# Strassen's method for the down products of two blocks, as a stage at the end of a layer kernel

## The chip, the cores and the metric

The kernel runs on one core of a Trainium2 chip. The metric is the time of one execution on the device in microseconds (us). A profiled execution shows the core's engines: TensorE (PE, with its weight loads as PEld), VectorE (DVE), ScalarE (ACT), GpSimd (POOL) and SyncE (SP), whose queue issues nearly all DMA transfers.

## The reference

One transformer layer on 2048 tokens of 640 features: a normalization, attention in a dilated window, a second normalization and a gated feed-forward layer with 1728 hidden features. Weights and data are float32.

```python
def _B_ref(x, w_gate, w_up, w_down):
    g = _silu(x @ w_gate)
    u = x @ w_up
    return (g * u) @ w_down

x = A_x
h = x + _A_ref(_layernorm(x, axis=-1), A_wqkv, A_wo)
h2 = h + _B_ref(_layernorm(h, axis=-1), B_w_gate, B_w_up, B_w_down)
return h2
```

`_A_ref` projects to queries, keys and values, attends for each token to 8 earlier positions two apart, and projects with `wo`.

## The kernel before, in words

The tokens are cut into four blocks of 512 (b = 0 to 3), the hidden features into 14 tiles of 128 (i = 0 to 13; the last has 64). Every float32 product is made from operands that are split into a high part, rounded for TensorE's faster float32 form (`fp32r`), and a low part, the difference. Three passes are multiplied and added up: high by high, low by high, high by low. A split costs a ScalarE cast (the high part) and a VectorE subtraction (the low part).

A feed-forward tile of one block is: gate and up products (5 chunks x 3 passes x 2 matmuls of 512 columns) into two banks of PSUM, SiLU on ScalarE, a multiply on VectorE, the split of the result (`act_split`), and the down product. The down product of a tile is 5 x 3 matmuls of 512 columns: four banks hold 128 tokens by 512 output features each, the fifth (bank 4) the last 128 features transposed. Banks 0 to 4 are accumulated over all 14 tiles of a block (`Downs` and `down_batch`), and `finish(b)` adds them to the residual `h_t()` and stores the block's output.

Blocks 0 and 1 go tile by tile (`ffn`, `classic`). Blocks 2 and 3 are done together in `pair(early)`, with `early` = 4:

- `wo3` makes block 3's attention output and its normalized input, which is moved into `kv`.
- Tiles 0 to 3 of block 2 are classic ones.
- `sums()` makes sums and differences of the two blocks' inputs. Tiles 4 to 12 are then `pair_tile`s: gate and up of both blocks from seven products in place of eight (Strassen's method over gate/up, the two blocks and two groups of chunks), in banks 5, 6 and 7 in turn. Block 2's activation goes on to its down product; block 3's is stored to the scratch tensor `psc`. `between()` puts a down batch of an earlier tile between the products.
- Tile 13 of block 2 is classic; `finish(2)`.
- For block 3, tiles 13 and 0 to 3 are classic ones. Tiles 4 to 12 are `kept_tile`s: the down weights are loaded again and split, the stored activation is loaded from `psc` and split, and the down product follows. Then `finish(3)`.

The order of all instructions is written out: every operation is recorded with `P.add(engine, cost, function, reads, writes, ...)`, and the table `ORDER` gives, in groups of (engine, first, count), the order in which they are emitted. Each engine executes its own in that order and waits by semaphores for those of others; DMA transfers are issued by SP in its order. The tile `ra` (19200 columns, fp32r) holds wo, weights and, in the pair stage, the sums; `wsl` (the space of `pq`), `kv`, `shb`, `acts` hold weights, block 3's input, block 2's input and the split activations, and `fa` float32 data.

```python
for i in range(early, NF - 1):
    d.put(pair_tile(i, fn[0], lambda: d.pend and d.do()))
    fn[0] += 1
```

## Time and profile before

| what | value |
|---|---|
| median of 3 runs | 850.06 us (847.94 to 850.62) |
| profiled execution | 849.7 us, span 848.0 us |
| TensorE busy | 839.8 us, 3953 matmuls |
| VectorE busy | 706.7 us, 847 instructions |
| ScalarE busy | 415.7 us, 745 instructions |
| DMA | 173.30 MB, mean 204 GB/s |
| HBM | read 126.57 MB, written 44.70 MB |

The span is the time from the first to the last instruction of the profiled execution; the rest of its time lies around it. Busy times are sums of the durations of instructions, and the durations of neighbours on an engine can overlap. The granted clock of TensorE is full in the whole span.

### The profile page before, as it was taken

To read this page: it belongs to the slowest core of one execution; us is meant where nothing else is said; L and a number is where in the kernel's file an instruction comes from. 1 tells how busy PE (TensorE), PEld (TensorE's weight loads), DVE (VectorE), ACT (ScalarE), POOL (GpSimd) and SP (SyncE) were. 2 spreads that over 40 slices of the span, in tenths; PEclk is the share of its full clock that TensorE was granted. 3 is DMA by queue.
4 is the path that set the end of the run, shared out by engine and by line. 5 is a ranking of instruction groups with operands and counts; after the bars stand their busy time and mean duration, and the time that the engine had idled before them with its cause. 6 is when DMAs were issued, how large, how long until landed. Compare 5 with 4: busy or idle time off the path is not lost.

```text
span 848.0 us, 10721 instructions
## 1 busy us (share of the span) xinstructions
PE 839.8 (99%) x3953; PEld 713.1 (84%) x3953; DVE 706.7 (83%) x847; ACT 415.7 (49%) x745; POOL 3.3 (0%) x12
## 2 busy tenths in 40 slices
PE   8999999999999999999999999999999999999998
PEld 7888888889888888887888888888878888888886
DVE  6499999999999999999999999996696667455343
ACT  6856574242872454477444457555553333234232
POOL 0000000000000000000000000000000000000000
PEclk9999999999999999999999999999999999999999
DMA  7897877658989795968999889868413122205332
GB/s 249 249 261 184 273 196 213 160 153 226 297 253 268 247 280 185 272 222 277 267 315 315 284 256 288 247 216 310 145 47 105 60 101 77 87 32 207 130 126 95
DMA packets 87141, 173.30 MB, mean 204 GB/s; under 512 B 33440, under 2 KB 52128, under 8 KB 86320
## 3 DMA queue, kind: packets, MB, share of 16 engines
q1 hardware_dynamic: 85680, 171.96, 66.0%
q10 hardware_dynamic: 1408, 0.66, 0.3%
q8 instruction: 31, 0.51, 0.2%
q14 instruction: 22, 0.18, 0.1%
HBM read 126.57 MB, written 44.70 MB: 202 GB/s over the span
## 4 chain that ended last, share of the span: by engine, by line
PE 72%; DVE 17%; DMA 4%; issue 2%; ACT 2%; SPq 1%; POOL 0%; DVEq 0%; ACTq 0%; POOLq 0%
PE bank L964 20%; PE bank L979 17%; PE bank L671 17%; PE bank L1132 12%; DVE pq L783 3%; DVE pq L742 3%; DVE pq L748 3%; PE bank L876 3%; DVE pq L792 2%; DMA pq<-qsc 2%; PE bank L1209 2%; DMA kv<-fa 1%; DMA kv<-ksc 1%; PE bank L528 1%; DMA ra<-lsc 1%
## 5 line engine op out<-in xcount | busy, mean ns | idle before, releaser
L964 PE MATMUL bank<-shb,ra 128*128 128x512 f32 x930 | 225.1, 390 | 0.1
L964 PEld LDWEIGHTS bank<-shb,ra 128*128 128x128 f32 x930 | 173.4, 188 | 35.7 <-DVE fa L1003 0.6
L979 PE MATMUL bank<-ra,acts 128*128 128x512 f32 x656 | 170.6, 390 | 0.2 <-DVE acts L1015 0.2
L979 PEld LDWEIGHTS bank<-ra,acts 128*128 128x128 f32 x656 | 122.3, 188 | 25.3 <-DVE acts L1015 0.6
L671 PE MATMUL bank<-ra,sha 128*128 128x512 f32 (+2 forms) x480 | 106.5, 380 | 0.2 <-ACT ra L642 0.2
L671 PE MATMUL bank<-ra,shb 128*128 128x512 f32 (+1 forms) x470 | 102.9, 378 | 0.0
L671 PEld LDWEIGHTS bank<-ra,sha 128*128 128x128 f32 x480 | 89.3, 188 | 13.4 <-ACT ra L642 0.5
L671 PEld LDWEIGHTS bank<-ra,shb 128*128 128x128 f32 x470 | 87.9, 188 | 12.7
L742 DVE TENSOR_TENSOR pq<-kv,pq 128x2560 f32<-128x2560 f32 x32 | 90.2, 2820 | 2.3 <-DMA pq<-qsc 1.3
L792 DVE TENSOR_TENSOR pq<-pq 128x1280 f32<-128x1280 f32 (+2 forms) x96 | 89.7, 934 | 2.0
L783 DVE TENSOR_TENSOR pq<-kv,pq 128x2560 f32<-128x2560 f32 x32 | 90.3, 2822 | 0.7
L748 DVE TENSOR_REDUCE pq<-pq 128x128 f32<-128x2560 f32 x32 | 90.0, 2811 | 0.4
L678 ACT ACTIVATE st<-bank,fa 128x480 f32<-128x480 f32 (+3 forms) x120 | 51.1, 473 | 52.3 <-PE bank L671 38.3
L940 DVE TENSOR_TENSOR ra<-fa,ra 128x640 fp32r<-128x640 f32 (+1 forms) x70 | 56.2, 819 | 13.3 <-ACT ra L930 12.1
L993 ACT CAST acts<-fa 128x512 fp32r<-128x512 f32 x52 | 32.1, 619 | 55.0 <-DVE fa L1003 41.6
L930 ACT CAST ra<-fa 128x640 fp32r<-128x640 f32 x56 | 40.4, 726 | 34.8 <-PE bank L979 34.8
L876 PE MATMUL bank<-ra 128*128 128x320 f32 x360 | 55.8, 309 | 0.0
L876 PEld LDWEIGHTS bank<-ra 128*128 128x128 f32 x360 | 54.3, 188 | 1.4
L945 ACT CAST ra<-fa 128x1280 fp32r<-128x1280 f32 (+1 forms) x35 | 42.5, 1216 | 21.9 <-DMA fa<-in_ffn_dram 17.6
L979 PE MATMUL bank<-acts,ra 128*128 128x512 f32 x164 | 45.9, 391 | 0.0
L1002 ACT ACTIVATE fa<-bank 128x512 f32<-128x512 f32 x34 | 20.3, 598 | 50.2 <-PE bank L964 47.0
L1003 DVE TENSOR_TENSOR fa<-bank,fa 128x512 f32<-128x512 f32 x34 | 23.2, 683 | 20.7 <-PE bank L964 10.9
(162 smaller groups left out, 969.4 us busy)
## 6 DMA issues: line engine op xcount, KB each, us to landing
fa<-in_ffn_dram SPq DMA_DIRECT2D x43, 960.0 KB, 6.1
kv<-ksc SPq DMA_DIRECT2D x32, 440.0 KB, 6.2
kv<-vsc SPq DMA_DIRECT2D x32, 440.0 KB, 6.2
ra<-lsc SPq DMA_DIRECT2D x17, 640.0 KB, 6.7
lsc<-ra SPq DMA_DIRECT2D x13, 640.0 KB, 7.1
ra<-lsc SPq DMA_DIRECT2D x19, 320.0 KB, 4.4
ksc<-st SPq DMA_DIRECT2D x32, 160.0 KB, 3.3
pq<-qsc SPq DMA_DIRECT2D x16, 320.0 KB, 6.8
```

The source lines that it names most:

```text
L671: T.matmul(banks[bk][:, 0:n], l, r_(wq(g, w, c) + shift, n), start=(p, c) == first_mm, stop=(p, c) == last_mm)
L678: P.add("ACT", act(m) + 0.06, lambda: A.activation(stage_t()[:, o : o + NJ * m].rearrange("p (t j c) -> p t j c", j=NJ, c=w)[:, :, j, :], ...
L742: P.add("DVE", dve(2560), lambda: V.tensor_tensor(pq(PROD, 2560).rearrange("p (j w c) -> p j w c", j=2, w=W), window(ko, 2 * jp), pq(qo + ...
L748: P.add("DVE", dve(2560), lambda: V.tensor_reduce(logits(lo)[:, :, 16 * jp : 16 * jp + 16].rearrange("p h n -> p n h"), pq(PROD, 2560).rea ...
L783: V.tensor_tensor(pq(PROD, 2560).rearrange("p (j n d) -> p j n d", j=2, d=DH), bass.AP(tensor=v.tensor, offset=v.offset, ap=[list(v.ap[0]) ...
L792: V.tensor_add(dst(v), v[:, :, 0:m, :], v[:, :, m : 2 * m, :])
L876: T.matmul(banks[bk][:, 0:320], l, r_(m, 320), start=p == 0 and c == 0, stop=p == 2 and c == NC - 1)
L940: low(640, lambda E, o=o: E.tensor_sub(ws(t, lo + o, 640)[p0:], fa[p0:, raw + o : raw + o + 640], ws(t, hi + o, 640)[p0:].bitcast(F32)), [ ...
L945: P.add("ACT", act(n), lambda: A.copy(ws(wt, gu, n), f(raw, n)), r=[rf(raw, n)], w=[rws(wt, gu, n)], prio=PR["fh"])
L964: T.matmul(banks[bk], ws(wt, gu + 1280 * w + wid * c + col, 128), x(a, c), start=p == 0 and c == 0, stop=p == 2 and c == NC - 1)
L979: T.matmul(banks[k], l, m, start=first and p == 0, stop=stop and p == len(passes) - 1)
L1132: T.matmul(banks[bk], ws(wt, o + 2048 * w + 128 * k, 128), xv_[k](a), start=first and p == 0 and k == 0, stop=stop and p == 2 and k == n - ...
```

## The change

The down products of eight tiles (4 to 11) of blocks 2 and 3 are taken out of the two blocks' accumulations and become the function `products(paired)` behind `finish(3)`.

- In the pair stage tile 12 now comes first, then the eight paired tiles. A paired tile (`keep`) loads only its gate and up weights, and its block-2 activation is stored to `psc[0]` instead of being split; block 3's goes to `psc[1]`, already in the order of the down product. Only tile 12 remains a `kept_tile`.
- `finish` of blocks 2 and 3 no longer stores the output; the new stage adds to `h_t()` and stores.
- `products` takes tiles in pairs (4 pairs). For each pair, the activations of both blocks form a 2 x 2 scheme (even or odd token rows j by first or second tile; each part 512 tokens by 128 features) and the down weights another (first or second tile by left or right 320 output features). Seven products with eight sums of parts for each pair (four of activations, four of weights) replace eight products. Each product (`m1` to `m7`) runs over the four pairs: `unit` splits one part of activations and one of weights into high and low (in a slot of a buffer that has become free), and `phase` issues 4 banks x 4 pairs x 3 passes of matmuls with 320 columns. `into` adds a bank to the output, and `store` sends it away. The float32 sources lie in `ar` (the first half of `ra`'s space) and `wr` (`shb`'s space); two small memsets on GpSimd mark when these become free.
- `ra` is cut into `ra` and `rb` of 9600 columns each, some offsets move by 128 columns, and `ORDER` is a new table for the whole program.

The diff without `ORDER` (of which two lines are shown) and small changes of names:

```diff
-EARLY = 4
+EARLY, NP = 4, 4
...
-    (2, 0, 1), (4, 2, 1), (3, 1, 1), (3, 0, 1), (4, 10, 1), (2, 7, 1), (1, 0, 1), (0, 0, 1), (4, 4, 1), (4, 3, 1), (1, 14, 1), (0, 1, 1), (0, 9, 1), (4, 5, 1),
+    (3, 1, 1), (3, 0, 1), (2, 0, 1), (0, 0, 1), (1, 0, 1), (4, 2, 1), (4, 7, 1), (2, 7, 1), (4, 4, 1), (0, 1, 1), (1, 10, 1), (4, 6, 1), (4, 5, 1), (0, 7, 1),
...
-        psc = dr.tile([NF, 128, 512], F32, name="psc")
+        psc = dr.tile([2, NF, 128, 512], F32, name="psc")
...
-            lo, hi = (n, n + 640) if cut else (0, n + 640)
+            lo, hi = ((0, n + 640), (n, n + 640), (0, n))[cut]
...
-            down_hi(raw, 1280, dn)
-            down_lo(i, raw, 1280, dn)
+            if not keep:
+                down_hi(raw, 1280, dn)
+                down_lo(i, raw, 1280, dn)
...
-            act_split(Y1, y1, ao, 2)
+            if keep:
+                P.add("SP", 0.45, lambda: Q.dma_start(psc[0, i], Y1()), r=[y1], w=[(f"R{i}", 0, 512)], prio=3, nbytes=nb(128, 2048))
+            else:
+                act_split(Y1, y1, ao, 2)
...
-            d = Downs(NF)
+            paired = list(range(early, early + 2 * NP))
+            others = [i for i in range(early, NF - 1) if i not in paired]
+            d = Downs(NF - 2 * NP)
...
-            for i in range(early, NF - 1):
-                d.put(pair_tile(i, fn[0], lambda: d.pend and d.do()))
+            for i in others + paired:
+                t = pair_tile(i, fn[0], lambda: d.pend and d.do(), i in paired)
+                if i in others:
+                    d.put(t)
                 fn[0] += 1
...
-            for i in range(early, NF - 1):
+            for i in others:
                 d.put(kept_tile(i))
...
             finish(3)
+            products(paired)
+
+        def products(ts):
+            n, m = len(ts), len(ts) // 2
+            S2, T2, Y1 = XN, AB2, AB2 + 1280
+            HN = 320
...
+            U = 1664
+            slots = [(lambda o=o: r_(o, U), [rr(o, U)]) for o in (17536,)]
+            slots += [(lambda o=o: kv[:, o : o + U], kvr(o, U)) for o in (0, U, 2 * U)]
+            slots += [(lambda o=o: r_(o, U), [rr(o, U)]) for o in (9600, 9600 + U)]
+            slots += [(lambda o=o: wsl_t()[:, o : o + U], [rpq(o, U)]) for o in (0, U, 2 * U)]
+            slots += [(lambda o=o: act_t()[:, o : o + U], [("ab", o, o + U)]) for o in (0, U)]
+            slots += [(lambda o=o: r_(o, U), [rr(o, U)]) for o in (13696, 13696 + U)]
+
...
+
+            def acts(s, odd):
+                v = lambda: ar_t()[:, 0 : 1024 * n].rearrange("p (b s jj o t) -> p b s jj o t", b=2, s=n, jj=2, o=2)[:, :, s, :, odd, :]
+                return v, [rr(512 * n * b + 512 * s + 256 * jj + 128 * odd, 128) for b in range(2) for jj in range(2)]
+
+            def wts(s, half):
+                o = 640 * s + HN * half
+                return (lambda: wr_t()[:, o : o + HN]), [("shb", o, o + HN)]
+
+            def s2(p):
+                return (lambda: f(S2 + 512 * p, 512).rearrange("p (b jj t) -> p b jj t", b=2, jj=2)), [rf(S2 + 512 * p, 512)]
+
+            def t2(p):
+                return (lambda: f(T2 + HN * p, HN)), [rf(T2 + HN * p, HN)]
+            P.add("POOL", 0.1, lambda: G.memset(ar_t()[:, RA_C - 2 : RA_C], 0.0), w=[rr(0, RA_C)], prio=0)
+            P.add("POOL", 0.1, lambda: G.memset(wr_t()[:, 0:2], 0.0), w=[("shb", 0, 5120)], prio=0)
+            for s, i in enumerate(ts):
+                for b in range(2):
+                    o = 512 * n * b + 512 * s
+                    P.add("SP", 0.45, lambda i=i, b=b, o=o: Q.dma_start(ar_t()[:, o : o + 512], psc[b, i]), r=[(f"{'RP'[b]}{i}", 0, 512)], w=[rr(o, 512)], prio=PR["fld"], nbytes=nb(128, 2048))
+                P.add("SP", 0.45, lambda i=i, s=s: Q.dma_start(wr_t()[:, 640 * s : 640 * s + 640], ffn_in[i][:, 1280:1920]), w=[("shb", 640 * s, 640 * s + 640)], prio=PR["fld"], nbytes=nb(128, 2560))
+            units = [0]
+
+            def unit(a, w):
+                k = units[0] % len(slots)
+                units[0] += 1
+                (av, ar), (wv, wr) = a, w
+                sv = slots[k][0]
+                for src, sr, o, c in ((av, ar, 0, 512), (wv, wr, 1024, HN)):
+                    hi, lo = (lambda o=o, c=c: sv()[:, o : o + c]), (lambda o=o, c=c: sv()[:, o + c : o + 2 * c])
+                    if c == 512:
+                        shape = lambda v: v.rearrange("p (b jj t) -> p b jj t", b=2, jj=2)
+                    else:
+                        shape = lambda v: v
+                    P.add("ACT", act(c), lambda src=src, hi=hi, shape=shape: A.copy(shape(hi()), src()), r=sr, w=part(k, o, c), prio=1)
+                    P.add("DVE", dve(c), lambda src=src, hi=hi, lo=lo, shape=shape: V.tensor_sub(shape(lo()), src(), shape(hi()).bitcast(F32)), r=sr + part(k, o, c), w=part(k, o + c, c), prio=1)
+                return k
+
+            def phase(us, bk0, first, stop):
+                for tp in range(4):
+                    for p, k in enumerate(us):
+                        def mm(tp=tp, p=p, k=k):
+                            v = slots[k][0]()
+                            for q, (a, w) in enumerate(((0, 0), (1, 0), (0, 1))):
+                                T.matmul(banks[bk0 + tp][:, 0:HN], v[:, 512 * a + 128 * tp : 512 * a + 128 * tp + 128], v[:, 1024 + HN * w : 1024 + HN * w + HN],
+                                         start=first and p == q == 0, stop=stop and p == m - 1 and q == 2, skip_group_check=True)
+                        P.add("PE", 3 * 0.1482, mm, r=part(k, 128 * tp, 128) + part(k, 512 + 128 * tp, 128) + part(k, 1024, 2 * HN), w=[pb(bk0 + tp)], prio=10)
+
+            def sub(o, x, y, add=False):
+                (ov, orr), (xv_, xr), (yv, yr) = o, x, y
+                c = 512 if len(orr) != 1 or orr[0][2] - orr[0][1] == 512 else HN
+                op = V.tensor_add if add else V.tensor_sub
+                P.add("DVE", dve(c), lambda: op(ov(), xv_(), yv()), r=xr + yr, w=orr, prio=1)
+
+            def into(tp, odd, half, bk):
+                b, j = tp // 2, 2 * (tp % 2) + odd
+                lo = 2560 * b + 640 * j + HN * half
+                P.add("DVE", dve(HN), lambda: V.tensor_add(h_t()[:, lo : lo + HN], banks[bk][:, 0:HN], h_t()[:, lo : lo + HN]), r=[pb(bk), ("sha", lo, lo + HN)], w=[("sha", lo, lo + HN)], prio=0.5)
+
+            def store(tp, odd, o, c):
+                b, j = tp // 2, 2 * (tp % 2) + odd
+                lo = 2560 * b + 640 * j + o
+                P.add("SP", 0.45, lambda: Q.dma_start(out[2 + b, :, j, o : o + c], h_t()[:, lo : lo + c]), r=[("sha", lo, lo + c)], prio=3, nbytes=nb(128, 4 * c))
+            ps = range(m)
+            m1 = [unit(acts(2 * p, 0), wts(2 * p, 0)) for p in ps]
+            m2 = [unit(acts(2 * p + 1, 0), wts(2 * p + 1, 0)) for p in ps]
+            phase(m1, 0, True, False)
+            for tp in range(4):
+                b, j = tp // 2, 2 * (tp % 2)
+                y = Y1 + HN * tp
+                P.add("ACT", act(HN), lambda y=y, tp=tp: A.copy(f(y, HN), banks[tp][:, 0:HN]), r=[pb(tp)], w=[rf(y, HN)], prio=0)
+                lo = 2560 * b + 640 * j + HN
+                P.add("DVE", dve(HN), lambda lo=lo, y=y: V.tensor_add(h_t()[:, lo : lo + HN], f(y, HN), h_t()[:, lo : lo + HN]), r=[rf(y, HN), ("sha", lo, lo + HN)], w=[("sha", lo, lo + HN)], prio=1)
+                lo = 2560 * b + 640 * j + 640
+                two = lambda v: v.rearrange("p (a c) -> p a c", a=2)
+                P.add("DVE", dve(640), lambda lo=lo, y=y, two=two: V.tensor_add(two(h_t()[:, lo : lo + 640]), f(y, HN)[:, None, :].to_broadcast([128, 2, HN]), two(h_t()[:, lo : lo + 640])),
+                      r=[rf(y, HN), ("sha", lo, lo + 640)], w=[("sha", lo, lo + 640)], prio=1)
+            phase(m2, 0, False, True)
+            for tp in range(4):
+                into(tp, 0, 0, tp)
+                store(tp, 0, 0, HN)
+            for p in ps:
+                a11, a21, a12, a22 = acts(2 * p, 0), acts(2 * p, 1), acts(2 * p + 1, 0), acts(2 * p + 1, 1)
+                b11, b12, b21, b22 = wts(2 * p, 0), wts(2 * p, 1), wts(2 * p + 1, 0), wts(2 * p + 1, 1)
+                sub(a11, a11, a21)
+                sub(b11, b12, b11)
+                sub(s2(p), a22, a11)
+                sub(t2(p), b22, b11)
+                sub(a21, a21, a22, True)
+                sub(a12, a12, s2(p))
+                sub(b12, b22, b12)
+                sub(b21, b21, t2(p))
+            m6 = [unit(s2(p), t2(p)) for p in ps]
+            phase(m6, 4, True, False)
+            for tp in range(4):
+                into(tp, 0, 1, 4 + tp)
+            m7 = [unit(acts(2 * p, 0), wts(2 * p, 1)) for p in ps]
+            phase(m7, 4, False, False)
+            for tp in range(4):
+                into(tp, 1, 1, 4 + tp)
+            m5 = [unit(acts(2 * p, 1), wts(2 * p, 0)) for p in ps]
+            phase(m5, 0, True, False)
+            for tp in range(4):
+                into(tp, 1, 1, tp)
+            m4 = [unit(acts(2 * p + 1, 1), wts(2 * p + 1, 0)) for p in ps]
+            phase(m4, 4, False, True)
+            for tp in range(4):
+                into(tp, 1, 0, 4 + tp)
+                store(tp, 1, 0, D)
+            m3 = [unit(acts(2 * p + 1, 0), wts(2 * p + 1, 1)) for p in ps]
+            phase(m3, 0, False, True)
+            for tp in range(4):
+                into(tp, 0, 1, tp)
+                store(tp, 0, HN, HN)
...
-                cuts = (0, 256, 512) if b == NB - 1 and j == NJ - 1 else (0, 512)
+                cuts = (0, 512)
...
+                    if b > 1:
+                        continue
```

```

Three places in the order, first TensorE in the middle of the pair stage, before. L1132 are the products of `pair_tile`, L979 down products; bank_74, bank_75 and bank_76 are banks 5, 6 and 7, bank_69 to bank_73 banks 0 to 4.

```order
L1132 MATMUL bank_74<-shb,wsl 128x512 x6
L1132 MATMUL bank_76<-kv,ra 128x512 x6
L979 MATMUL bank_71<-ra,acts 128x512 x3
L1132 MATMUL bank_75<-ra,wsl 128x512 x6
L979 MATMUL bank_73<-acts,ra 128x512 x3
L1132 MATMUL bank_76<-kv,ra 128x512 x3
L1132 MATMUL bank_75<-ra,wsl 128x512 x6
L1132 MATMUL bank_75<-kv,wsl 128x512 x3
```

The same engine and stage after the change, where L1158 are the products of `pair_tile`, and bank_75, bank_76, bank_77 are banks 5, 6 and 7 (bank_70 to bank_74 are banks 0 to 4).

```order
L1158 MATMUL bank_75<-shb,wsl 128x512 x6
L1158 MATMUL bank_76<-ra,wsl 128x512 x6
L1158 MATMUL bank_77<-ra,wsl 128x512 x6
L1158 MATMUL bank_76<-ra,wsl 128x512 x6
L1158 MATMUL bank_76<-kv,wsl 128x512 x3
L1158 MATMUL bank_75<-shb,wsl 128x512 x9
L1158 MATMUL bank_76<-ra,wsl 128x512 x9
L1158 MATMUL bank_75<-shb,rb 128x512 x6
L1158 MATMUL bank_76<-ra,rb 128x512 x6
```

The down products have gone from between; only six matmuls on bank 5 or 7 lie between two uses of bank 6.

TensorE at the passage to the new stage, after the change: L1004 are down products, L1405 the new products, L1482 `finish`'s transposes.

```order
L1004 MATMUL bank_71<-rb,acts 128x512 x3
L1405 MATMUL bank_77<-wsl 128x320 x3
L1004 MATMUL bank_70<-rb,acts 128x512 x3
...
L1004 MATMUL bank_73<-rb,acts 128x512 x6
L1405 MATMUL bank_70<-rb 128x320 x3
L1004 MATMUL bank_74<-acts,rb 128x512 x6
L1405 MATMUL bank_70<-kv 128x320 x3
L1405 MATMUL bank_71<-rb 128x320 x3
L1405 MATMUL bank_71<-kv 128x320 x3
L1482 MATMUL bank_74<-fa 128x128 x4
```

Before, the same engine ended in down products alone:

```order
L979 MATMUL bank_71<-ra,acts 128x512 x6
L1316 MATMUL bank_73<-fa 128x128 x4
L979 MATMUL bank_69<-ra,acts 128x512 x6
L979 MATMUL bank_70<-ra,acts 128x512 x6
L979 MATMUL bank_72<-ra,acts 128x512 x9
```

The new products begin between the last down products of block 3 and go on for 336 matmuls.

VectorE at that passage, after the change: L1396 are the low parts of `unit`, L1413 the sums of parts, L1489 `finish`'s additions, L965 and L1022 the splits of down weights and activations, L1028 the gate-up multiply of a classic tile.

```order
L1028 TENSOR_TENSOR fa<-bank_76,fa 128x512
L1396 TENSOR_TENSOR kv<-ar,kv 128x512
L1413 TENSOR_TENSOR ar<-ar 128x2x2x128
L1396 TENSOR_TENSOR kv<-ar,kv 128x512
L1396 TENSOR_TENSOR kv<-wr,kv 128x320
L1413 TENSOR_TENSOR ar<-ar 128x2x2x128 x2
L965 TENSOR_TENSOR rb<-fa,rb 128x640
L1022 TENSOR_TENSOR acts<-fa,acts 128x4x4x32
L965 TENSOR_TENSOR rb<-fa,rb 128x640
L1022 TENSOR_TENSOR acts<-fa,acts 128x512
L1396 TENSOR_TENSOR rb<-wr,rb 128x320
```

And before, behind the last gate-up multiply (L1003; L997 and L940 split activations and down weights):

```order
L1003 TENSOR_TENSOR fa<-bank_75,fa 128x512
L997 TENSOR_TENSOR acts<-fa,acts 128x4x4x32 x2
L940 TENSOR_TENSOR ra<-fa,ra 128x640
L997 TENSOR_TENSOR acts<-fa,acts 128x4x4x32
L940 TENSOR_TENSOR ra<-fa,ra 128x640
```

Where two splits alternated for each kept tile, the units and sums of the new stage now stand among the splits of the last tiles, and go on behind them.

44 lines of the change are left out of this document (29 added, 15 removed), and 442 rows, old and new, of the table ORDER.

## The prediction

> **What bounds the kernel now.** I read the page first, then the chain that ended last, the windows of the last 250 us, and the groups of that stretch.
>
> ```profile
> span 848.0 us, 10721 instructions
> PE 839.8 (99%) x3953; PEld 713.1 (84%) x3953; DVE 706.7 (83%) x847; ACT 415.7 (49%) x745; POOL 3.3 (0%) x12
> PEclk9999999999999999999999999999999999999999
> PE 72%; DVE 17%; DMA 4%; issue 2%; ACT 2%; SPq 1%; POOL 0%; DVEq 0%; ACTq 0%; POOLq 0%
> ```
>
> TensorE is busy 99% of the span at full granted clock, so its work sets the time, wherever nothing makes it wait. A busy matmul is longer than the step to the next one, because they overlap; the price of a matmul is its share of a run in the chain of waits:
>
> ```profile
> 492.04 2.19 PE bank L876 x15
> 578.02 0.88 PE bank L1209 x6
> 806.29 32.64 PE bank L979 x144
> 838.93 0.44 PE bank L1316 x4
> ```
>
> A 128x512 down product (L979) steps at 32.64 / 144 = 0.2267 us, a 128x320 product (L876) at 2.19 / 15 = 0.1460 us; six of L1209 give 0.147, the same. These two are the terms of the sum.
>
> VectorE is the second engine. It has room only in the late windows (columns: window, length, then busy time and instruction count of PE, PEld, DVE, ACT, POOL):
>
> ```profile
> 650.00:700.00 50.00, 50.00 (x222) 41.32 (x221) 30.52 (x49) 17.14 (x27) 0.00 (x0) 1.00 0.25 89
> 740.00:760.00 20.00, 20.00 (x90) 16.57 (x89) 9.30 (x14) 6.08 (x10) 0.63 (x1) 1.00 0.00 1
> 780.00:800.00 20.00, 20.00 (x89) 16.54 (x89) 8.25 (x12) 6.01 (x8) 0.00 (x0) 1.00 0.49 172
> 820.00:830.00 10.00, 10.00 (x46) 8.29 (x45) 4.31 (x6) 3.75 (x6) 0.00 (x0) 1.00 0.53 173
> ```
>
> From 740 us on, VectorE and ScalarE are busy less than half of the time and the DMA engines about half. That idle time is what the change spends.
>
> **The change, part by part.** *Matmuls removed.* Eight tiles, two blocks, 5 banks x 3 passes: 8 x 2 x 15 = 240 products of 512 columns, 240 x 0.2267 = 54.40 us of TensorE.
>
> *Matmuls added.* Seven products, 4 banks each, 4 pairs of tiles, 3 passes: 7 x 4 x 4 x 3 = 336 of 320 columns, 336 x 0.1460 = 49.06 us. TensorE saves 5.34 us. In columns it is exactly 7/8 (107520 for 122880), but the step is not in proportion to columns: 320/512 of 0.2267 would be 0.1417, so the narrower shape gives back 336 x 0.0043 = 1.4 us. The Trainium skill (TensorE: Matmul & The Clock Gate, "Wait — 56ns, not 53.3ns?") gives a warm step of columns over 2.4 GHz plus about 2.5 ns; by that the saving would be an estimated 240 x 215.8 - 336 x 135.8 ns = 6.2 us. The trace disagrees: its two steps make (0.2267 - 0.1460) / 192 = 0.42 ns a column and a fixed 11 ns, and the rows count.
>
> *Vector and Scalar work removed.* Each of the eight tiles drops, in the pair tile and again in the kept tile, the down weights' cast and difference and the activations' cast and difference:
>
> ```profile
> L940 DVE TENSOR_TENSOR ra<-fa,ra 128x640 fp32r<-128x640 f32 x27 | 21.9, 822 | 13.2 <-ACT ra L930 12.1 <-ACT ra L945 1.1
> L997 DVE TENSOR_TENSOR acts<-fa,acts 128x512 fp32r<-128x512 f32 x26 | 17.8, 688 | 13.7 <-ACT acts L993 13.7
> L930 ACT CAST ra<-fa 128x640 fp32r<-128x640 f32 x28 | 20.1, 724 | 16.6 <-PE bank L979 16.6
> L993 ACT CAST acts<-fa 128x512 fp32r<-128x512 f32 x26 | 16.0, 618 | 16.4 <-PE bank L979 10.1 <-DVE fa L1003 3.0 <-DVE fa L1106 1.8
> L1256 DVE TENSOR_TENSOR h<-bank,h 128x320 f32<-128x320 f32 x8 | 3.9, 485 | 2.7 <-PE bank L1209 2.5
> L1219 ACT COPY fa<-bank 128x320 f32<-128x320 f32 x6 | 2.6, 426 | 7.7 <-PE bank L1209 7.7
> ```
>
> That is 16 x (0.822 + 0.688) = 24.2 us of VectorE and 16 x (0.724 + 0.618) = 21.5 us of ScalarE; none of it was on the path, so it earns nothing by itself.
>
> *Vector and Scalar work added.* 28 units split activations and weights into high and low parts (28 x 512 and 28 x 320 columns on each engine), 32 sums and differences (16 x 512, 16 x 320), and the additions to the result (28 x 320, 4 x 640; ScalarE copies 4 x 320). VectorE: 44 x 0.688 + 72 x 0.485 + 4 x 0.82 = 68.5 us by duration; ScalarE 28 x 0.618 + 32 x 0.426 = 30.9 us. They must run inside the last 100 us, beside TensorE. Whether they fit depends on the step from one VectorE instruction to the next, not on its duration (three pairs in order of time: start, length; then two groups that the pair stage needs below):
>
> ```profile
> 654.20 0.42 DVE L1108 TENSOR_TENSOR fa<-fa 128x256 f32<-128x256 f32 x1
> 654.53 0.69 DVE L997 TENSOR_TENSOR acts<-fa,acts 128x512 fp32r<-128x512 f32 x1
> 785.19 0.82 DVE L940 TENSOR_TENSOR wsl<-fa,wsl 128x640 fp32r<-128x640 f32 x1
> 785.92 0.69 DVE L1003 TENSOR_TENSOR fa<-bank,fa 128x512 f32<-128x512 f32 x1
> 786.52 0.82 DVE L940 TENSOR_TENSOR wsl<-fa,wsl 128x640 fp32r<-128x640 f32 x1
> L1146 DVE TENSOR_TENSOR fa<-bank,fa 128x512 f32<-128x512 f32 x9 | 6.2, 689 | 6.3 <-PE bank L1132 6.1
> L1111 DVE TENSOR_TENSOR ra<-fa,ra 128x1024 fp32r<-128x1024 f32 x5 | 6.1, 1221 | 0.5 <-ACT ra L1110 0.5
> ```
>
> 640 columns step at 785.92 - 785.19 = 0.73, 512 at 0.60, 256 at 0.33; 320 between them, which I put at 0.40. So an instruction's last 0.085 us lie under its successor.
>
> Now the stretch that decides. I start both engines at the last gate and up products of block 3 (the last L1028 multiply in VectorE's order). Behind it stand on TensorE 69 products of 512 (downs of the tiles left), 4 transposes and the 336: 69 x 0.2267 + 0.44 + 49.06 = 65.1 us (0.44 is the row of L1316). On VectorE stand 45 instructions of 512, 66 of 320 and 6 of 640 columns: 45 x 0.60 + 66 x 0.40 + 6 x 0.73 = 57.8 us by steps, 45 x 0.688 + 66 x 0.485 + 6 x 0.822 = 67.9 us by durations. Thirteen of the new instructions stand ahead of that point. Walking both sums through the order, VectorE by steps is ready at least 2.4 us before TensorE wants each operand or bank; near the end, where it waits for a bank itself, the lead is some 0.4 us. By durations it is up to 5.7 us late (at the first matmuls of the last phase). I take the steps, since these rows are the same kinds of instruction; the durations are the upper end.
>
> *Pair stage.* Products of gate and up use banks 5, 6 and 7 in turn; before, three matmuls of a down product stood between many of them and covered the emptying of a bank. Now a paired tile has none. In the order I count 22 places where only six matmuls (1.36 us) lie between the last write of a bank and its next write after one eviction; before there were 6. Evictions last 0.69 us (L1146), and VectorE has less else to do there. The whole stage before shows idle time at its start alone:
>
> ```profile
> 616.98 1.67 PE L1132 MATMUL bank<-shb,ra 128*128 128x512 f32 x6 [0.63 <-ACT fa L1144]
> 620.03 2.55 PE L1132 MATMUL bank<-ra 128*128 128x512 f32 x10 [0.21 <-DVE ra L1066]
> 624.73 1.63 PE L1132 MATMUL bank<-ra 128*128 128x512 f32 x6 [0.80 <-DVE fa L1146]
> L1132 PE MATMUL bank<-ra,wsl 128*128 128x512 f32 x108 | 26.9, 389 | 0.0
> ```
>
> 1.64 us in three waits, while the sums of block 3's input were late; the six places with 1.36 us of cover ran without a wait. So I price the 22 at zero, cover 1.36 - 0.69 = 0.67 us each.
>
> *DMA and queues.* Gone: the down weights in the pair tiles' loads (8 x 320 KB), 8 loads of 320 KB and 8 of 256 KB in the kept tiles. New: 8 stores of 256 KB (the block-2 activations), 24 loads into the freed activation and weight buffers, all through SP's one queue, and block 2's output now leaves at the end with block 3's, in 12 stores. In SP's order the weight loads follow the last use of block 2's input by a matmul, the activation loads the last sums, and between them stand the raw-weight loads of the last classic tiles; a store waiting for a multiply holds up what is behind it.
>
> ```profile
> fa<-in_ffn_dram SPq DMA_DIRECT2D x9, 320.0 KB, 2.8
> fa<-psc SPq DMA_DIRECT2D x9, 256.0 KB, 3.3
> psc<-fa SPq DMA_DIRECT2D x9, 256.0 KB, 2.1
> ```
>
> 24 x 3 us would be 73 us one after the other, but up to eight are under way together, and some 45 us of matmuls stand between the first load and the first phase: zero on the path. The two GpSimd memsets only release the buffers. If the loads were late, ScalarE's casts would be the first to wait.
>
> *Tail.* Before, the last bank is added in two instructions:
>
> ```profile
> 844.20 0.76 DVE L1323 TENSOR_TENSOR h<-bank,h 128x256 f32<-128x256 f32 x2 [1.35 <-PE bank L979]
> ```
>
> Now it is one of 320 columns (0.485 us) and a slightly larger store (160 for 128 KB): zero, within -0.3 to +0.3. *The rest of the order* is new throughout: at the start, TensorE's transposes for three rows stand ahead of the first QKV product instead of two. Same instructions; zero, within 0.5 us either way.
>
> *Sum.* -5.34 for matmuls; waits of TensorE between -1.64 (the three gone) and +5.7 (VectorE by durations). I take +0.6: the order keeps a lead everywhere, so I expect about a third of what entering the pair stage cost. Together -4.7. The profiled execution took 849.7 us for its span of 848.0; it becomes 845.0. The median of the runs, 850.06, lies 0.36 above it, so 845.3.
>
> **Rivals.** *A, the forecast*: TensorE stays the bound; 843.3 to 847.2 with the waits from -1.6 to +2.4.
>
> *B, VectorE bounds the last stage.* If its instructions step nearer to their durations, because they follow each other's results or wait for a cast just done, TensorE waits up to 5.7 us: 849.7 - 5.3 + 5.7 + 0.36 = 850.4, no change. For it: 67.9 against 65.1 us, and chains such as the sums that feed one another. Against: the steps above. It begins to show when the steps are on average some 0.03 us longer (2.4 us over about 100 instructions). The Trainium skill (VectorE: DVE Perf Modes, "The DRAIN you can't avoid") says that the next Vector instruction does not start until the pipeline is empty, and advises to keep the count of instructions down. By that rule this rival would hold; the trace disagrees, 0.60 us from start to start at 0.69 us of duration.
>
> *C, the other side: banks of the pair stage.* If each of the 22 places cost what the worst row at the stage's start did, 0.80 us, that is 17.6 us: 850.06 - 5.34 + 17.6 = 862.3. It ends slower than before from (5.34 + 2.55) / 22 = 0.36 us a place. For it: a 1.22 us VectorE instruction (L1111) in front of an eviction eats the 0.67 us of spare cover. Against: no wait in the group of 108, and the order puts evictions first.
>
> **How the numbers follow.** A 0.66, B 0.20, C 0.08; 0.06 for something better than A (below 843.3). A difference of 0.3%, 2.55 us, is about what a measurement of this kernel can tell. A is faster whole (to 847.5), B spreads from 847 to 851 and gives some 0.05 to faster, 0.13 to same and 0.02 to slower; C is slower, save 0.02. Faster 0.77, same 0.14, slower 0.09. The range takes A whole and most of B: 843.0 to 849.6; A's own is 843.3 to 847.2.
>
> **What would show it.** Right: 336 matmuls of 320 columns at 0.146 us a step, no idle time of TensorE above 1 us in all in the pair stage and the last stage, VectorE busy near 750 us. B shows as idle time ahead of the new products, released by VectorE; C as idle time ahead of the pair tiles' matmuls, released by evictions; late loads as ScalarE waiting for DMA ahead of the new casts. The forecast is wrong if TensorE's waits grow by more than 2.8 us, wherever.

## The result and the profile after

The changed kernel takes 842.34 us (median of 11 runs, 840.82 to 846.90), the kernel before 848.87 (median of 11, 847.76 to 850.62): ratio 0.9923, 95% interval 0.9906 to 0.9941, a gain of 6.5 us (5.0 to 8.0). The forecast was 845.3, with a range from 843.0: the direction was right, the gain was larger than forecast (4.7), and the time lies 0.66 us below the range.

The page of the changed kernel:

```profile
span 843.4 us, 11052 instructions
PE 835.2 (99%) x4049; PEld 717.4 (85%) x4049; DVE 744.5 (88%) x934; ACT 426.3 (51%) x774; POOL 3.4 (0%) x14
```

TensorE has 96 matmuls more (336 - 240) and is still busy 99%; VectorE has 38 us more. Its waits of TensorE (time in all, times, longest):

```profile
PE bank L568 <- POOL rb L1508: 1.9, 1, 1.9
PE bank L901 <- ACT fa L904: 0.9, 1, 0.9
PE bank L989 <- DVE fa L1028: 0.7, 2, 0.5
PE bank L989 <- ACT fa L1027: 0.6, 1, 0.6
PE bank L641 <- DVE fa L515: 0.5, 1, 0.5
PE bank L1004 <- DVE acts L1040: 0.3, 1, 0.3
```

No line of the pair stage (L1158) and none of the new stage (L1405) is among them: the last wait listed lies ahead of 560 us. The three waits of L1132, 1.64 us, are gone. What waits is the work ahead of the pair stage, called the front from here on, and this one execution was on the slow side: it took 845.2 us, the second longest of the 11. A second profile of the same kernel took 841.7 (span 839.9), and beside the first wait, which both kernels have, its list of waits has none:

```profile
PE bank L568 <- POOL rb L1508: 1.9, 1, 1.9
```

The chain of the second profile, from the first uninterrupted run of the new products (start, length), and then the tail, VectorE's last addition:

```profile
789.61 47.09 PE bank L1405 x321
836.69 0.02 issue
836.72 0.49 DVE h L1418
```

321 products of 320 columns step at 47.09 / 321 = 0.1467 us. From the start of the last addition to the end of the span it takes 839.9 - 836.72 = 3.18 us.

The list of waits counts idle time from the modelled end of a matmul, 0.39 us behind its start, while the next one of 512 columns normally starts 0.2267 us behind it. So it leaves out the first 0.16 us of each delay, and its smallest entries are 0.2 us. What TensorE loses is read better from the starts, and this text calls it "lost by the starts": the time from one start to the next, less the usual step of that shape.

### The profile page after: what moved, and what is told of

It reads as the page before. It is cut to its first block, busy times and chain, and to the rows that moved or that the text cites. A ratio compares the mean times of both kernels' runs of the same rounds, so it can differ in the third digit from the quotient of the medians.

```text
span 843.4 us, 11052 instructions
## 1 busy us (share of the span) xinstructions
PE 835.2 (99%) x4049; PEld 717.4 (85%) x4049; DVE 744.5 (88%) x934; ACT 426.3 (51%) x774; POOL 3.4 (0%) x14
## 5 line engine op out<-in xcount | busy, mean ns | idle before, releaser
L989 PE MATMUL bank<-shb,rb 128*128 128x512 f32 x930 | 227.0, 390 | 1.4 <-DVE fa L1028 0.7
L989 PEld LDWEIGHTS bank<-shb,rb 128*128 128x128 f32 x930 | 173.2, 188 | 38.4 <-DVE fa L1028 2.1
L1004 PE MATMUL bank<-rb,acts 128*128 128x512 f32 x464 | 121.4, 391 | 0.0
L1004 PEld LDWEIGHTS bank<-rb,acts 128*128 128x128 f32 x464 | 86.4, 188 | 17.3
L767 DVE TENSOR_TENSOR pq<-kv,pq 128x2560 f32<-128x2560 f32 x32 | 90.2, 2819 | 3.2 <-DMA pq<-qsc 1.9
L808 DVE TENSOR_TENSOR pq<-kv,pq 128x2560 f32<-128x2560 f32 x32 | 90.3, 2821 | 1.3 <-DMA kv<-vsc 0.7
L901 PE MATMUL bank<-ra 128*128 128x320 f32 x360 | 55.9, 309 | 0.9 <-ACT fa L904 0.9
L901 PEld LDWEIGHTS bank<-ra 128*128 128x128 f32 x360 | 54.2, 188 | 2.7 <-ACT fa L904 1.3
L696 PE MATMUL bank<-ra,sha 128*128 128x480 f32 (+2 forms) x240 | 53.6, 380 | 0.0
L696 PE MATMUL bank<-rb,sha 128*128 128x512 f32 (+1 forms) x240 | 52.6, 378 | 0.0
L696 PE MATMUL bank<-ra,shb 128*128 128x512 f32 (+1 forms) x240 | 52.0, 378 | 0.0
L696 PE MATMUL bank<-rb,shb 128*128 128x512 f32 (+1 forms) x230 | 50.8, 379 | 0.0
L696 PEld LDWEIGHTS bank<-rb,sha 128*128 128x128 f32 x240 | 44.9, 188 | 6.4
L696 PEld LDWEIGHTS bank<-ra,sha 128*128 128x128 f32 x240 | 44.5, 188 | 6.6 <-ACT sha L643 0.2
L965 DVE TENSOR_TENSOR rb<-fa,rb 128x640 fp32r<-128x640 f32 (+1 forms) x54 | 43.4, 818 | 1.3 <-DMA lsc<-rb 0.7
L1027 ACT ACTIVATE fa<-bank 128x512 f32<-128x512 f32 x34 | 20.3, 598 | 42.4 <-PE bank L989 38.4
```

Source lines behind the costliest of these rows:

```text
L696: T.matmul(banks[bk][:, 0:n], l, r_(wq(g, w, c) + shift, n), start=(p, c) == first_mm, stop=(p, c) == last_mm)
L767: P.add("DVE", dve(2560), lambda: V.tensor_tensor(pq(PROD, 2560).rearrange("p (j w c) -> p j w c", j=2, w=W), window(ko, 2 * jp), pq(qo + ...
L808: V.tensor_tensor(pq(PROD, 2560).rearrange("p (j n d) -> p j n d", j=2, d=DH), bass.AP(tensor=v.tensor, offset=v.offset, ap=[list(v.ap[0]) ...
L901: T.matmul(banks[bk][:, 0:320], l, r_(m, 320), start=p == 0 and c == 0, stop=p == 2 and c == NC - 1)
L965: low(640, lambda E, o=o: E.tensor_sub(ws(t, lo + o, 640)[p0:], fa[p0:, raw + o : raw + o + 640], ws(t, hi + o, 640)[p0:].bitcast(F32)), [ ...
L989: T.matmul(banks[bk], ws(wt, gu + 1280 * w + wid * c + col, 128), x(a, c), start=p == 0 and c == 0, stop=p == 2 and c == NC - 1)
```

## Experiments

Theory W says: the gain is the matmuls, the waits at the start of the pair stage, and the tail. Its rivals: F, the re-made order of the front gives part of it; O, the order of TensorE at the start of the pair stage does; and B and C of the prediction, on how near VectorE and the banks are to being the bound.

**Both kernels again.**

> The kernel before, unchanged, for a second profile. Theory W (the three waits at the start of the pair stage belong to the kernel: block 3's input reaches kv late for the sums): the profile shows TensorE waiting there again, 1.2 to 2.2 us in all for L1132. Rival R (they were an accident of that one execution): under 0.3 us. Both: time within 0.3% of 848.9.

> The changed kernel, unchanged, for a second profile. Its first profile took 845.2 us with about 4 us of waits ahead of the pair stage, while the median of its runs is 842.3. Theory W: waits in the pair stage and the last stage stay under 0.5 us in all, and those ahead of the pair stage fall to about 2.5 us in a run of 842 to 843. Rival R: the pair stage waits again for 1 us or more. Rival B of the prediction (VectorE): more than 1 us of waits for L1405.

Measured 848.67 (ratio 1.0001, 0.9991 to 1.0010) and 843.01 (0.9930, 0.9916 to 0.9945). Of the kernel before, the second profile (span 847.1) has this wait in the pair stage:

```profile
PE bank L1132 <- DVE fa L1146: 0.8, 1, 0.8
```

and its chain ends in this addition:

```profile
843.27 0.42 DVE h L1323
```

The wait is there again, though 0.8 us by this view, less than the 1.2 expected; the other two of the first profile are not listed. The starts in TensorE's timeline say more:

```profile
622.17 0.84 PE L1132 MATMUL bank<-shb,ra 128*128 128x512 f32 x3
623.79 1.62 PE L1132 MATMUL bank<-ra 128*128 128x512 f32 x6 [0.78 <-DVE fa L1146]
625.25 0.86 PE L979 MATMUL bank<-ra,acts 128*128 128x512 f32 x3
```

Three matmuls take 1.62 us to the next start in place of 0.68, and the six behind the wait 1.46 in place of 1.36; a delay of 0.3 us a little earlier is in no list. Added up over single matmuls from 600 to 640 us, 1.4 us are lost by the starts here and 2.4 in the first profile, where the list gave 1.64. The tail is 847.1 - 843.27 = 3.83 us, against 3.18 after the change. The two spans differ by 7.2 us. Neither profile of the changed kernel lists a wait in the pair stage or in the last stage.

**The fronts exchanged.** The order ahead of the pair stage from the one kernel, the rest from the other; the first line of the table shows it, here for the changed kernel with the old front:

```diff
-    (3, 1, 1), (3, 0, 1), (2, 0, 1), (0, 0, 1), (1, 0, 1), (4, 2, 1), (4, 7, 1), (2, 7, 1), ...
+    (2, 0, 1), (4, 2, 1), (3, 1, 1), (3, 0, 1), (4, 10, 1), (2, 7, 1), (1, 0, 1), (0, 0, 1), ...
```

> The changed kernel with the instructions ahead of the pair stage (blocks 0 and 1, attention) in the order that the kernel before had; the pair stage and the new stage as changed. Theory W (the gain is 5.3 of matmuls, 1.6 to 2.1 of waits at the start of the pair stage and 0.6 at the tail, and the front is neutral): 841.5 to 843.5. Rival F (the re-made order of the front gives the 1.8 us that the prediction did not have): 844 to 845, and the waits ahead of the pair stage are 1.5 us more.

> A second profile of the changed kernel with the old order ahead of the pair stage. If the re-made front of the changed kernel is the more easily disturbed one (its profiles lost 0.4 to 4.1 us between 420 and 520 us), this one loses under 1 us there again; time 841.5 to 843.

> The kernel before with the instructions ahead of the pair stage in the order that the change has; everything behind is as before. Theory W: 848 to 850, no difference from before. Rival F: 846.5 to 847.5.

> A second profile of the kernel before with the re-made order ahead of the pair stage, which took 853.0 where both theories had expected 850 or less. If its waits belong to the front: TensorE loses 2 us or more between 280 and 600 us beyond the 2.1 us of the kernel before. If they come at the passage into the pair stage: 2 us or more beyond it between 600 and 640 us.

The changed kernel with the old front took 842.62 (0.9929, 0.9917 to 0.9941), and the second time 843.55 (0.9944, 0.9930 to 0.9957): no faster and hardly slower than with its own. The second time is 0.5 us above what was expected, and its interval reaches rival F's 844. As F had it, more waits are listed ahead of the pair stage (3.4 us, for 1.9 in the second profile of the changed kernel). But 1.0 us of them is a wait that neither kernel has there, and both profiles of this exchange show it at the very matmul where the two orders meet:

```profile
PE bank L1025 <- DVE acts L1061: 1.2, 2, 1.0
```

So the exchange makes a cost of its own, and the traces decide better than the times: up to 520 us, 3.9 to 6.1 us are lost by the starts in the six profiles with the old front and 3.2 to 7.4 in the eight with the new one, those of the later experiments included. No gain from the new front shows in this scatter, and rival F has nothing left for it. The kernel before with the new front took 853.00 (1.0049, 1.0036 to 1.0062), and the second time 849.97 (1.0019, 1.0007 to 1.0030). Neither theory had the first, and the two don't agree with each other. Both profiles (spans of 848.8 and 846.8 us) list a wait of 0.8 us just behind the place where the orders meet (L1228), but they are of the quickest executions of their runs and don't show where the rest of the time goes. This stays open. It speaks against a gain from the new front all the same.

What the expectation on disturbed fronts asked can be read from VectorE's waits in 420 to 520 us. In the changed kernel's first profile:

```profile
DVE pq L767 <- DMA kv<-ksc: 0.8, 1, 0.8
DVE pq L808 <- DMA kv<-vsc: 0.7, 1, 0.7
```

In the profile of `load_ahead` (below) with the same front:

```profile
DVE pq L788 <- DMA kv<-ksc: 3.0, 1, 3.0
```

In the second profile of the changed kernel there is no such wait; with the old front it was 0.3 us. VectorE is busy 94 to 98% of that stretch, and the profiles with the longer waits for keys are those in which TensorE loses more there: 4.0 us by the starts in `load_ahead`, 2.3 in the first profile, 0.3 in the second. This may be where the 6 us between the changed kernel's fastest and slowest runs come from; no run tried it, and that the new order is more exposed to it is only suggested by these few profiles.

**What made TensorE wait at the start of the pair stage.** Before the change, the second profile has these transfers of block 3's input into `kv` (duration of the issues, first and last start), from both queues, and the time from issue to landing:

```profile
L1275 SPq DMA_DIRECT2D kv<-fa x8: 602/615/1104, 600.6 to 606.0; - x8
L1275 ACTq DMA_DIRECT2D kv<-fa x8: 592/619/827, 600.6 to 606.9; - x8
DMA to landing us min/median/max: 2.2/2.7/5.6
```

SP's timeline goes on behind them with:

```profile
606.72 0.53 SPq L926 DMA_DIRECT2D fa<-in_ffn_dram  x1
```

This is the load of the next pair tile's weights, 960 KB, issued at 606.72, ahead of the last input transfer on ScalarE's queue (606.9). That one transfer is the slow one, and the chain that ended last runs through it to the sums and to TensorE's wait:

```profile
606.95 5.56 DMA kv<-fa
```

In the first profile it is the same: the load at 607.14, the transfer at 607.38, 6.07 us to landing. The expectation that follows puts the load behind the last transfer; that is so on SP's queue alone. The experiment all but takes the load away: 16 columns of 1920 are left, and the tile multiplies what an earlier load left there.

```diff
             lo, hi = (n, n + 640) if cut else (0, n + 640)
+            if rn[0] - 1 == 33:
+                hi = 16
```

> The kernel before, with the load of the second pair tile's weights cut from 960 KB to 16 columns a row; that tile computes with weights that an earlier load left there. This load is issued 0.1 us behind the last transfer of block 3's input into kv, whose last pieces then take up to 6.1 us to land (3.7 after the change). Theory W (that load shares the DMA engines with the input, the sums come late, and TensorE waits 1.5 to 2.5 us at the start of the pair stage): the input lands within 4 us, the waits there fall under 0.6 us, and the time to 847 to 848. Rival O (the waits come from the order of TensorE and VectorE there: pair products begin while down products of earlier tiles are still to come): the input lands sooner, and TensorE still loses 1.2 us or more there; 848.9, no change.

Measured 847.40 (0.9983, 0.9973 to 0.9993): 1.4 us faster than before. The landing of the same transfers in that run:

```profile
DMA to landing us min/median/max: 2.1/2.5/3.9
```

And in the second profile of the changed kernel, the transfers on ScalarE's queue and the landing of all:

```profile
L1304 ACTq DMA_DIRECT2D kv<-fa x8: 597/615/1907, 598.7 to 604.7; - x8
DMA to landing us min/median/max: 2.1/2.5/4.0
```

With the load gone the input lands within 3.9 us, no wait of TensorE is listed in the pair stage, and 0.05 us are lost by the starts between 600 and 640 us. Theory W holds for the kernel before, and rival O, which had 1.2 us or more still lost there, falls: the collision with that load cost about 1.4 us (0.6 to 2.3 by the interval). The next three kernels ask what of the change took it away.

```diff
 DMA kv<-fa 32x5x128 x8
+DMA fa<-in_ffn_dram 128x1280
 DMA rb<-lsc 128x640
-DMA fa<-in_ffn_dram 128x1280 x4
+DMA fa<-in_ffn_dram 128x1280 x3
```

> The changed kernel with two loads exchanged in SP's order: the second pair tile's weights (640 KB) now come directly behind block 3's input, ahead of the 320 KB of down weights that held the queue until 607 us. Theory W: the input lands up to 2 us later and TensorE loses 0.3 to 1.5 us at the start of the pair stage; 842.6 to 844.2. Rival O: no wait there (under 0.2 us), 842.3 to 843.0.

Measured 844.30 (0.9934, 0.9919 to 0.9950), above what either theory had by the median but not apart from the changed kernel's 0.9930, and no wait in the pair stage; the 4.0 us lost between 420 and 520 us, above, are ahead of the edit. The transfers on ScalarE's queue, the landing of all, and then the load in SP's timeline:

```profile
L1325 ACTq DMA_DIRECT2D kv<-fa x8: 592/620/1314, 602.8 to 608.9; - x8
DMA to landing us min/median/max: 2.1/3.0/4.0
```

```profile
609.91 0.53 SPq L972 DMA_DIRECT2D fa<-in_ffn_dram  x1
```

The load is now right behind SP's last input transfer, and the input still lands within 4.0 us: W's expectation of a later landing failed. The difference from before is ScalarE's queue. Its last transfer is issued 1.0 us ahead of the load here, and 0.2 us behind it before the change. So what counted is not the neighbour in SP's order but that the input's last pieces, on the other queue, came after the load. That is inferred from these rows; ScalarE's order was not tried by itself, nor was the size of the load, which after the change is 640 KB in place of 960.

The order of TensorE, in the kernel before (L979 down products, L1132 pair products):

```diff
 L979 MATMUL bank_70<-ra,acts 128x512 x3
-L1132 MATMUL bank_74<-shb,ra 128x512 x6
 L979 MATMUL bank_72<-ra,acts 128x512 x3
 L979 MATMUL bank_69<-ra,acts 128x512 x3
 L979 MATMUL bank_71<-ra,acts 128x512 x3
 L979 MATMUL bank_73<-acts,ra 128x512 x3
-L1132 MATMUL bank_74<-shb,ra 128x512 x6
+L979 MATMUL bank_70<-ra,acts 128x512 x3
+L979 MATMUL bank_69<-ra,acts 128x512 x3
+L1132 MATMUL bank_74<-shb,ra 128x512 x12
 L979 MATMUL bank_72<-ra,acts 128x512 x3
 L1132 MATMUL bank_75<-ra 128x512 x6
 L1132 MATMUL bank_76<-ra 128x512 x6
-L979 MATMUL bank_70<-ra,acts 128x512 x3
```

> The kernel before, with six down products (18 matmuls, 4.1 us) that stood between or behind the first pair products put ahead of them in TensorE's order, as the change has them; the splits that they need move up with them. The 960 KB load stays where it was. Theory W (the late input is what costs): the sums are as late as before, and only the 1.36 us of the two products that had stood behind the sums' first use cover a part: TensorE still loses 0.3 us or more there, 848 to 848.7. Rival O (the order of TensorE alone explains the waits): under 0.2 us lost, 847 to 848.

Measured 851.53 (1.0029, 1.0017 to 1.0040), slower by 2.5 us, which neither theory had. Its waits in the pair stage (L1152 are the pair products, L1164 the copy out of bank 5):

```profile
PE bank L1152 <- ACT fa L1164: 2.5, 1, 2.5
PE bank L1152 <- DVE fa L1166: 0.5, 1, 0.5
```

The edit set two uses of bank 5 next to each other, and ScalarE's copy out of the bank stands behind casts that wait for the input. Since the run made a new wait, it says nothing on the size of W's, and it decides nothing about O either; `small_load` does that. In the changed kernel the same two down products were put behind the first sums:

```diff
-L1004 MATMUL bank_71<-rb,acts 128x512 x3
-L1004 MATMUL bank_70<-rb,acts 128x512 x3
 L1004 MATMUL bank_74<-acts,rb 128x512 x3
 L1158 MATMUL bank_75<-shb,rb 128x512 x6
 L1158 MATMUL bank_76<-ra,rb 128x512 x6
+L1004 MATMUL bank_71<-rb,acts 128x512 x3
 L1158 MATMUL bank_75<-shb,rb 128x512 x6
+L1004 MATMUL bank_70<-rb,acts 128x512 x3
 L1158 MATMUL bank_76<-ra,rb 128x512 x6
```

> The changed kernel, with two down products (6 matmuls, 1.36 us) put back behind the first products of the sums, as the kernel before has them; the sums are needed 1.36 us earlier. Theory W (after the change the sums are ready early, because the input lands early): at most 0.7 us of waits there (the low part of T2 ends 0.72 us ahead of its product), 842.3 to 843.4. Rival O: 1.2 us or more of waits, above 843.5.

Measured 842.89 (0.9936, 0.9918 to 0.9953): no listed wait between 600 and 640 us, 0.3 us lost there by the starts, no slowing that the times could show. With the input in time the order of those products matters little.

**How near rivals C and B were.** The evictions of bank 6 twice:

```diff
-lambda: V.tensor_add(Y2(), banks[b_], Y1())
+lambda: [V.tensor_add(Y2(), banks[b_], Y1()) for _ in range(2)]
```

and the same for `Y3`.

> The changed kernel, in which two of the evictions of bank 6 in each pair tile (18 in all) are issued twice, with the same result, so that the bank comes free one 128x512 VectorE step (0.60 us) later. The prediction's cover (1.36 us of matmuls less an eviction of 0.69 leave 0.67 us): no more than 1 us of new waits, below 844. Rival C of the prediction (the cover is used up by what stands ahead of the eviction): up to 18 x 0.6 = 10.8 us, 846 to 853, as waits of L1158 for VectorE.

Measured 848.30 (0.9995, 0.9984 to 1.0006): 5.5 us more than the changed kernel's 0.9930. The first and the last piece of the pair products in TensorE's timeline (start, length), first of the changed kernel's second profile, then of this one.

```profile
616.04 1.52 PE L1158 MATMUL bank<-shb,rb 128*128 128x512 f32 x6
731.80 2.20 PE L1158 MATMUL bank<-kv,rb 128*128 128x512 f32 x9
```

With the evictions doubled:

```profile
617.98 1.52 PE L1158 MATMUL bank<-shb,rb 128*128 128x512 f32 x6
740.09 2.20 PE L1158 MATMUL bank<-kv,rb 128*128 128x512 f32 x9
```

Its waits:

```profile
PE bank L1158 <- DVE fa L1172: 1.6, 7, 0.2
PE bank L1158 <- DVE fa L1179: 0.2, 1, 0.2
```

From the one to the other it is 115.76 us, and 122.11 here: 6.35 us more. So it is neither the 0 to 1 of the cover nor C's whole 10.8. One of the places, first VectorE and then TensorE:

```profile
648.07 1.41 DVE L1172 TENSOR_TENSOR fa<-bank,fa 128x512 f32<-128x512 f32 x2
647.09 2.20 PE L1158 MATMUL bank<-shb,rb 128*128 128x512 f32 x9
649.53 1.66 PE L1158 MATMUL bank<-ra,rb 128*128 128x512 f32 x6 [0.24 <-DVE fa L1172]
```

The two additions take 1.41 us where one takes 0.69: a second one that writes the same tile starts only when the first has ended, so the edit added 0.72 us a place, not the 0.60 of the expectation. TensorE's nine matmuls would have ended their steps at 649.13; the next starts at 649.53, 0.40 us late. By the starts, 12 of the 18 places are late by 0.2 to 0.4 us, each with another 0.1 us in the matmul behind, and six show nothing. At 11 of the 12 the cover that was left is 0.72 less 0.3 to 0.4, so 0.3 to 0.4 us, not 0.67.

VectorE in the last stage:

```diff
-lambda ...: V.tensor_sub(shape(lo()), src(), shape(hi()).bitcast(F32))
+lambda ..., t=2 if 8 <= units[0] - 1 < 12 else 1: [V.tensor_sub(...) for _ in range(t)]
```

> The changed kernel with the eight low parts of the third product (m6) of the new stage computed twice: 4 x (0.60 + 0.40) = 4.0 us more of VectorE by steps, 4.7 by durations, in the middle of the last stage. By the prediction's steps VectorE leads there by 2.4 us or more: 0 to 1.6 us of waits ahead of L1405, 842.5 to 844.5. Rival B (VectorE is all but the bound): the whole 4 to 4.7 us, 846.5 to 847.

Measured 845.65 (0.9959, 0.9947 to 0.9972), 2.5 us more than 0.9930 by the medians. The last stage by itself: the first new products and the last ones, first in the changed kernel's second profile:

```profile
777.93 0.60 PE L1405 MATMUL bank<-wsl 128*128 128x320 f32 x3
836.08 0.60 PE L1405 MATMUL bank<-kv 128*128 128x320 f32 x3
```

With the low parts of m6 twice:

```profile
779.90 0.60 PE L1405 MATMUL bank<-wsl 128*128 128x320 f32 x3
841.67 0.60 PE L1405 MATMUL bank<-kv 128*128 128x320 f32 x3
```

Its largest waits there:

```profile
PE bank L1405 <- ACT kv L1395: 0.9, 1, 0.9
PE bank L1405 <- DVE acts L1396: 0.5, 1, 0.5
PE bank L1405 <- DVE h L1418: 0.4, 1, 0.4
```

And two pieces of its chain, which runs through VectorE there and then through TensorE without a break:

```profile
808.14 0.60 DVE rb L1396
808.74 0.40 DVE h L1418
809.14 0.40 DVE h L1433
...
812.53 29.75 PE bank L1405 x201
```

It is 58.15 us without and 61.77 with the added work: 3.6 us come out at the end. More than the expected 4.0 were added, since each doubled low part takes as long as two that wait for one another:

```profile
797.20 1.41 DVE L1396 TENSOR_TENSOR acts<-fa,acts 128x512 fp32r<-128x512 f32 x2
801.66 1.01 DVE L1396 TENSOR_TENSOR acts<-fa,acts 128x320 fp32r<-128x320 f32 x2
```

That is 0.72 and 0.52 us more than one, 5.0 in all; 1.25 of it disappears in idle time that VectorE has ahead of its last gate-up multiply (1.30 and 0.83 us there without, 0.78 and 0.10 with). So the difference does not give the lead, but the last wait says where to look. It has 201 of the 336 products behind it. In the second profile of the changed kernel, the addition that this wait is for and the first of the 201 products are:

```profile
806.28 0.49 DVE L1418 TENSOR_TENSOR h<-bank,h 128x320 f32<-128x320 f32 x1
807.04 0.60 PE L1405 MATMUL bank<-kv 128*128 128x320 f32 x3
```

The addition ends at 806.77, 0.27 us ahead of the product. That is VectorE's lead in the middle of the stage, where the expectation's 0 to 1.6 had counted on the prediction's 2.4 us; it was wrong. The changed kernel stands just on the good side of rival B.

## Why the prediction was right or wrong

*Base.* 1.2 of the 3.0 us between 845.3 and 842.34 is the base: it was taken from the three runs shown (850.06), and eleven give 848.87. The other 1.8 are the effect, 6.5 for 4.7.

*Matmuls: right.* Predicted -5.34, measured 54.4 - 336 x 0.1467 = -5.1. The new shape steps at 0.1467 where 0.1460 was used. It is also not the estimated 0.1358 of the Trainium skill's page ("TensorE: Matmul & The Clock Gate", "Wait — 56ns, not 53.3ns?"), so the rows of the old kernel were the better source.

*Waits: the step that failed.* The prediction named the three waits that would go (1.64 us) and then put +0.6 for the new ones, as "about a third of what entering the pair stage cost". The order gave no such wait, and the new stage has none in either profile of the changed kernel. The term should have been near the lower end of its own range: removing what made the old waits is worth 1.4 us by `small_load`. Its 1.64 was also a sum of listed idle times, for which 2.4 us are lost by the starts in that profile and 1.4 in the next. It was not worked out what caused them. The trace of before had it: the input landed late beside a 960 KB load, and the new order issues the input's last pieces ahead of that load, which is also a third smaller.

*Tail: mis-sized.* Predicted zero, within 0.3; measured 3.80 and 3.83 before, 3.19 and 3.18 after: -0.64. Two additions of 256 columns became one of 320, as priced, and what is left of the 0.64 lies between that addition and the end of the store.

*Sum.* -5.1 - 1.4 - 0.64 = -7.1; the two later profiles differ by 7.2, the medians by 6.5. What is left is small beside the front, where executions differ by up to 4 us.

*Range.* By its own terms A's lower end is 850.06 - 5.34 - 1.64 = 843.1, not 843.3, and with the lower ends of the tail (-0.3) and of the order (-0.5), which the range leaves out, 842.3. (24 loads of 3 us are 72 us, not 73; nothing rests on that.)

*VectorE (B): right, but by luck as to the margin.* VectorE steps at 0.60 and 0.40 us (the estimate for 320 columns came out), and by steps it fits, with 0.27 us to spare at the place that the added work found. The walk through the order had 0.4 us near the end and at least 2.4 us for that place; a margin a tenth of the one counted on was enough. By the sentence of the Trainium skill that the prediction uses ("VectorE: DVE Perf Modes", "The DRAIN you can't avoid") the durations 0.688 and 0.485 would add up, and the chain above disagrees with it again. But the same section adds that a next instruction that is not held starts earlier, which the prediction left out and with which these rows agree. A second instruction that writes what the first wrote does wait for its end: 0.72 us behind a start for 512 columns, 0.52 for 320. That is the step B feared of instructions that follow each other's results; a few pairs of the new work take it too (0.73 us from 768.40 to 769.13 in the second profile), but too few to make VectorE the bound.

*Banks (C): right result, cover too large.* No wait is listed at the 22 places, as priced. But the "1.36 - 0.69 = 0.67 us" of cover was 0.3 to 0.4 where `evict_twice` found it: a last matmul is busy 0.389 us, not a step of 0.227, so the bank is full 0.16 us later than counted. Some 0.04 us from a matmul's end to the start of an addition that waits for it, and 0.05 from the addition's end to the next matmul, both read from that run's trace, leave an estimated 0.42; an eviction that other VectorE work holds up has less.

*Loads, stores and GpSimd: right*, zero on the path: no wait of TensorE in the last stage in which they could show.

## What to carry to other kernels

A wait that stands in the profile of before has a cause; find it before deciding whether a change keeps it. Here a large load had delayed a small urgent transfer on another queue, and its going was worth 1.4 us beside the 5.1 of the matmuls. When an engine's work is traded for another's, compare their sums of steps, not of durations, and then test the lead by adding work to the second engine. Read from the trace how much was added: an instruction done twice into the same tile took more than twice the step here. Cover for a bank is counted from the end of the last matmul, not from the end of its step, and it can be measured by making the eviction longer.

## What the runs showed that was not expected

TensorE loses more than its list of waits says: with 1.8 us of waits listed for bank evictions, `evict_twice` lost 6.35. About 0.16 us of every delay lies under the end of the matmul before it and is not counted as idle, delays that leave less than about 0.15 us of idle time are not listed at all, and the matmul behind a wait takes some 0.34 us to the next start in place of 0.227. And a median of three runs of this kernel can lie 1.2 us off the median of eleven, a quarter of the effect that was forecast.
